# Layer hand-over of a two-layer decode kernel: a four-place weight ring, 36 instead of 72 reloaded blocks of V61, and a written-out order for layer 0's last two heads

## Chip, cores and metric

The kernel runs on one NeuronCore of a Trainium2 chip. The metric is the device time of one execution in microseconds. The engines are named as in the profile: PE (matrix multiply), PEld (its weight loads), DVE (vector), ACT (scalar), POOL (GpSimd) and SP (the queue that issues the DMAs).

## What is computed

One decode step (one token, batch 2) through two layers. Each layer is attention with 32 heads over a cache of 16384 positions, head size 128, and a small mixer with an MLP of width 4608 on a model width of 576. Both layers use the same weights and the same K and V caches.

```python
def _A_ref(x, k_cache, v_cache, wq, wo):
    q = (x @ wq).reshape(B, Sq, H, Dh).transpose(0, 2, 1, 3)
    scores = jnp.einsum("bhqd,bhkd->bhqk", q, k_cache) * (Dh ** -0.5)
    p = _softmax(scores, axis=-1)
    o = jnp.einsum("bhqk,bhkd->bhqd", p, v_cache)
    return o.transpose(0, 2, 1, 3).reshape(B, Sq, H * Dh) @ wo
...
    h = _gelu(_layernorm(x) @ w1)                 # four quarters, each shifted along the sequence
    hs = jnp.concatenate([g0, g1, g2, g3], axis=-1) @ w2
    x1 = x + hs
    return x1 + _gelu(_layernorm(x1) @ w3) @ w4

x = x + _A_ref(_layernorm(x), A_k_cache, A_v_cache, A_wq, A_wo)
x = x + _B_ref(_layernorm(x), B_w1, B_w2, B_w3, B_w4)
```

The last two lines are executed twice. With one position the shifted quarters are zero, so `hs` does not depend on x. K and V of one batch entry and head are 4 MB each; there are 64 such units, so a layer reads 512 MB of caches beside some 20 MB of weights.

## The kernel before

A unit u is one batch entry and head. Its K and V tiles are [128 partitions, 128 blocks of 128 values], 32 KB a partition. SBUF holds six such slots (`mem`); a slot is refilled as soon as the work on its old tile is done. `Store` is the planner: every transfer has a fixed address and a fixed place in one list, and `pump` issues the list strictly in order on SP, each when its address range is free.

For each unit the scores come in two ways. Half of the blocks go through PE: eight blocks (a chunk) are transposed into a PSUM buffer (`transposes`, L1246; four buffers `tps`), ACT copies them to SBUF (`evacuate`, L1258), and PE multiplies them with the query (`scores`, L1272). The other half goes through DVE: a product with the broadcast query and a sum, 16 blocks at a time (`dots`, L1292 and L1296). Then come the maximum (`softmax_max`, with an all-reduce on POOL, L1312), the exponential on ACT (`softmax_exp`), and the product with V on PE in four groups of 32 blocks (`pv`, L1366). `landed` puts a semaphore increment on POOL's queue that waits for a tile's DMA and lets PE go on; POOL runs these in program order with the all-reduces. Units 2 to 61 are a hardware loop over three units a turn; units 62 and 63 and everything between the layers are straight-line code.

Between the layers not everything is read again. Layer 1 begins with units 62, 63 and 61 (`order`): K62, V62, K63, V63 and K61 stay in SBUF, and of V61 the blocks from `GONE` on. The space of V61's first 72 blocks (four places of 576 KB, `a`) and of K61's first 36 (two places, `c`) is the ring through which wo, w3, w4 of layer 0 and wq of layer 1 are streamed: 36 pieces, most of 576 KB, wq's of 512 KB, two of w4's of 288 KB. When PE has multiplied a piece, its place is free for the piece that comes next in that place. After wq, V61's first blocks are loaded again in four pieces, then K of unit 0.

So that K62 and K63 serve layer 1 without DVE, their halves that DVE used are transposed in place (`turn`, 16 chunks: eight transposes and one evacuation each). K61's first five chunks are parked before the ring takes their space (`park`): three evacuated into the `kt` buffers, two left in PSUM buffers. Before the change four turned chunks lie in unit 63's attention and the first three parkings behind its pv of unit 62; the other twelve turns and two parkings lie between the weight pieces, after the pieces that the table `TURNS` names, and two ahead of the gelu:

```python
TURNS = {("w3", 0): 1, ("w3", 1): 1, ("w3", 2): 1, ("w4", 1): 1, ("w4", 3): 1, ("w4", 6): 1, ("w4", 8): 1,
         ("wq", 0): 1, ("wq", 1): 1, ("wq", 2): 1}
```

The order of the work between the layers is: the end of attention (`totals`, normalisation), wo (`rows_projection`, L877), layernorm (matmul of its sums L698), w3 (`cols_chunk`, L754; two of its five chunks of rows need no layernorm; tail L771), gelu, w4 (L877), layernorm, wq (L754, tail L771), and layer 1's first heads (`carried`).

Of the kernel before, what the change touches and what calls it, by code (L numbers as in the profile page):

```python
# [328 lines left out]
class KB:  # L329
    NL = 2  # L330
    CH = 8
# [6 lines left out]
    NS = 3  # L338
# [160 lines left out]
    def plan_all(self):  # L499
# [145 lines left out]
    def layer(self, l):  # L645
# [16 lines left out]
        if l == 0:  # L662
            self.turn(2, settle=False)
        self.gelu_z()
        self.settle()
# [77 lines left out]
    def cols_chunk(self, w, l, k, out, pk, n, rhs, rk, cols, first, last=False, held=False):  # L743
# [53 lines left out]
    def q_projection(self, l):  # L797
# [7 lines left out]
                       after=lambda: self.cols_chunk("wq", l, 0, acc, [ak], n, self.raw[:, 0, 0:w], "raw", cols, True, True, True))  # L805
        if l:
            self.settle()
# [56 lines left out]
    def rows_projection(self, w, l, rhs, rk):  # L864
# [4 lines left out]
        for i, (a, b, _) in enumerate(cuts):  # L869
# [16 lines left out]
            if l == 0:  # L886
                if (w, i) == ("wo", 1):
                    self.park(self.order(0)[self.U - self.CARRY - 1], self.NKT, self.PARKED)
                self.turn(self.TURNS.get((w, i), 0))

    def z_projection(self, l):
# [6 lines left out]
        chunk = lambda k: self.cols_chunk("w3", l, k, acc, [ak], MT, self.raw[:, k, :], "raw", cols, k == 0, k == R - 1, k > 0)  # L898
        chunk(0)
        self.layernorm("x1", self.x1, self.xn, "xn", after=lambda: chunk(1))  # L900
        if l == 0:
            self.settle()
# [28 lines left out]

    def still(self, l, s):

        return l == 0 and s >= self.U - self.CARRY
# [19 lines left out]
    def attention(self, l):  # L954
# [11 lines left out]
        for s in range(self.CARRY + 1 if l else 0, U):  # L966
            if s == enter:
                first = self.g.mark()
            if s == leave:
                self.g.loop(first, (leave - enter) // NS)  # L970
# [55 lines left out]
        while pend:  # L1026
            self.scores(*pend.pop(0))
# [438 lines left out]
```

## Time and profile before

| | |
|---|---|
| time, median of 3 runs (lowest to highest) | 2549.78 us (2549.26 to 2550.42) |
| the profiled execution: its time, its span | 2550.04 us, 2548.1 us |
| read from HBM | 1092.37 MB, 429 GB/s over the span |
| busy share PE, DVE, ACT, POOL | 63%, 74%, 47%, 2% |
| TensorE clock granted, mean | 0.574 |

The page of the profile counts busy time by engine, cuts the span into 40 equal slices of 63.7 us (a digit is the busy share in tenths, below them the GB/s that the DMA engines moved), follows the chain of work that ended last, and lists the costliest groups of instructions and the DMA issues with the time from issue to landing. The hand-over between the layers lies at about 1223 to 1345 us, in slices 20 to 22. Views of a window take the same trace for a stretch: busy time per engine, the instructions in order of time, who waited for whom.

### The profile page before, as it was taken

The page shows a single profiled execution, that of the slowest core. Times are in us where ns is not written, and L with a number is a line of the kernel's source. Part 1 is how long each engine was busy: PE and PEld are TensorE (multiplying, and loading weights), DVE is VectorE, ACT ScalarE, POOL GpSimd, SP SyncE. Part 2 cuts the span into 40 slices and gives each one's busy share as a digit, 9 for nine tenths or more (in the row PEclk, how much of TensorE's full clock was granted, in tenths as well). Part 3 has the DMA queues.
Part 4 walks back from the last instruction along what each step waited for, and adds up shares of the span by engine and source line. Part 5 has one row for each costly group of instructions (what it writes and reads, how often), then busy time and mean ns, then how long its engine had stood idle before and what let it go on. Part 6 is the DMA issues. An engine that isn't in the chain of part 4 may idle for free.

```text
span 2548.1 us, 74895 instructions
## 1 busy us (share of the span) xinstructions
PE 1614.3 (63%) x34407; PEld 1580.3 (62%) x34407; DVE 1896.9 (74%) x2061; ACT 1204.4 (47%) x1812; POOL 53.5 (2%) x151
## 2 busy tenths in 40 slices
PE   4666666656666666666767766666665666666566
PEld 3666666656665665666667756666665666666566
DVE  5877777777777777777638877777777777777774
ACT  3544544444454444445435544444454445444442
POOL 0000000000000000000000000000000000000000
PEclk8555555555555555555655555555555555555555
DMA  9999999999999999999999999999999999999999
GB/s 411 427 432 432 432 433 431 432 432 432 432 430 433 430 434 431 434 430 434 417 410 430 430 432 431 434 431 431 433 430 434 430 433 430 434 431 434 431 433 386
DMA packets 46928, 1093.19 MB, mean 429 GB/s; under 512 B 5140, under 2 KB 6296, under 8 KB 12440
## 3 DMA queue, kind: packets, MB, share of 16 engines
q1 hardware_dynamic: 46872, 1092.40, 100.0%
q8 instruction: 41, 0.67, 0.1%
q14 instruction: 15, 0.12, 0.0%
HBM read 1092.37 MB, written 0.00 MB: 429 GB/s over the span
## 4 chain that ended last, share of the span: by engine, by line
DMA 66%; DVE 23%; PE 5%; issue 5%; SPq 1%; ACT 0%; DVEq 0%; POOLq 0%
DMA mem<-in_A_k_cache_dram 63%; DVE s_dve L1296 12%; DVE prod L1292 9%; PE tps L1246 2%; PE mps L1366 2%; DMA mem<-in_B_w_dram 1%; DMA mem<-in_A_wo_dram 1%; PE sps L1272 1%; SPq L101 1%; PE sps L1217 1%; DVE diag L1213 0%; DMA mem<-in_A_wq_dram 0%; DVE l L1344 0%; DVE q_col L1210 0%; DVE mx L1307 0%
## 5 line engine op out<-in xcount | busy, mean ns | idle before, releaser
L1258 ACT ACTIVATE kt<-tps 128x1024 bf16<-128x1024 bf16 x992 | 1002.7, 1023 | 878.4 <-PE tps L1246 860.3
L1296 DVE TENSOR_REDUCE s_dve<-prod 128x16 f32<-128x2048 bf16 x504 | 1152.1, 2286 | 17.3
L1246 PE MATMUL tps<-ident,mem 128*128 128x128 bf16 x8192 | 999.4, 300 | 141.6 <-POOLq L202 135.2
L1292 DVE TENSOR_TENSOR prod<-mem,qb 128x2048 bf16<-128x2048 bf16 x504 | 616.8, 1224 | 525.0 <-POOLq L202 493.8
L1366 PE MATMUL mps<-p,mem 128*128 128x1 bf16 x16384 | 512.2, 165 | 549.9 <-POOLq L202 520.0
L1246 PEld LDWEIGHTS tps<-ident,mem 128*128 128x128 bf16 x8192 | 761.1, 136 | 151.6 <-POOLq L202 144.9
L1366 PEld LDWEIGHTS mps<-p,mem 128*128 128x128 bf16 x16384 | 487.6, 104 | 558.4 <-ACT p L1327 552.3
L1272 PEld LDWEIGHTS sps<-q_col,kt 128*128 128x128 bf16 x7936 | 399.1, 113 | 0.6 <-ACT kt L1258 0.5
L1272 PE MATMUL sps<-q_col,kt 128*128 128x1 bf16 x7936 | 387.6, 170 | 0.2
L1217 PE MATMUL sps<-diag,ones_bf 128*128 128x128 bf16 x127 | 36.4, 287 | 195.3 <-DVE diag L1213 195.3
L1217 PEld LDWEIGHTS sps<-diag,ones_bf 128*128 128x128 bf16 x127 | 13.2, 104 | 205.6 <-DVE diag L1213 205.6
L1321 ACT ACTIVATE mx<-mx 128x1 f32<-128x1 f32 x128 | 26.0, 203 | 235.9 <-POOL mx L1312 235.9
L1312 POOL PARTITION_ALL_REDUCE mx<-mx x128 | 51.1, 399 | 2442.2 <-DVE mx L1310 2323.5
L1220 ACT ACTIVATE qb<-sps 128x128 bf16<-128x128 f32 x127 | 35.2, 277 | 137.7 <-PE sps L1217 137.7
L1324 ACT ACTIVATE p<-s_dve,mx 128x64 bf16<-128x64 f32 x126 | 43.8, 348 | 4.1
L1258 ACT ACTIVATE mem<-tps 128x1024 bf16<-128x1024 bf16 x32 | 32.0, 1025 | 21.9 <-PE tps L1246 19.5
L1327 ACT ACTIVATE p<-sps,mx 128x64 bf16<-128x64 f32 x128 | 37.7, 294 | 0.1
L1307 DVE TENSOR_REDUCE mx<-sps 128x1 f32<-128x64 f32 x128 | 27.7, 216 | 7.3 <-PE sps L1272 7.2
L1213 DVE TENSOR_SCALAR diag<-ident,q_f 128x128 bf16<-128x128 bf16 x127 | 31.1, 245 | 0.0
L877 PE MATMUL mps<-prod,mem 128*128 128x2 bf16 x680 | 22.2, 166 | 14.1 <-DMA mem<-in_B_w_dram 8.3
L877 PEld LDWEIGHTS mps<-prod,mem 128*128 128x128 bf16 x680 | 20.6, 104 | 15.9 <-DMA mem<-in_B_w_dram 7.0
L710 ACT ACTIVATE misc<-misc 128x2 f32<-128x2 f32 x8 | 2.4, 296 | 51.8 <-DVE misc L708 51.8
(116 smaller groups left out, 293.7 us busy)
## 6 DMA issues: line engine op xcount, KB each, us to landing
mem<-in_A_k_cache_dram SPq DMA_DIRECT2D x124, 4096.0 KB, 40.7
mem<-in_A_v_cache_dram SPq DMA_DIRECT2D x123, 4096.0 KB, 49.6
mem<-in_B_w_dram SPq DMA_DIRECT2D x21, 576.0 KB, 7.8
mem<-in_B_w_dram SPq DMA_DIRECT2D x7, 1152.0 KB, 33.8
mem<-in_A_v_cache_dram SPq DMA_DIRECT2D x3, 2048.0 KB, 40.4
mem<-in_A_wq_dram SPq DMA_DIRECT2D x10, 512.0 KB, 6.6
mem<-in_A_wo_dram SPq DMA_DIRECT2D x8, 576.0 KB, 19.2
mem<-in_A_wq_dram SPq DMA_DIRECT2D x4, 1024.0 KB, 8.0
```

The costliest lines, as they stand in the source:

```text
L877: ins = pe.matmul(self.mps[:, t * B:(t + 1) * B], lhsT=buf[:, o:o + 128], rhs=rhs(k), start=(k == 0 and t == 0), stop=(k == last), skip_gr ...
L1217: self.pe(lambda pe: pe.matmul(qps, lhsT=self.ones_bf[:, :], rhs=self.diag[:, :], start=True, stop=True, skip_group_check=True), reads=["o ...
L1220: self.act(lambda e: e.activation(out=self.qb[i][:, :], in_=qps, func=ACT.Copy), reads=[("qps", i)], writes=[("qb", i)], sig=("qb", i))
L1246: ins = pe.transpose(self.tps[t][:, j * 128:(j + 1) * 128], buf[:, j * 128:(j + 1) * 128], self.ident[:, :])
L1258: self.act(lambda e: e.activation(out=out, in_=self.tps[t][:, :], func=ACT.Copy), reads=[("tps", t)], writes=keys, sig=("evac", c, t, k))
L1272: ins = pe.matmul(self.sps[sp][:, c * self.CH + j:c * self.CH + j + 1], lhsT=buf[:, j * 128:(j + 1) * 128], rhs=self.q_col[:, sp:sp + 1], ...
L1292: self.dv(lambda e: e.tensor_tensor(out=prod, in0=buf.rearrange("p (j d) -> p j d", d=128), in1=qbc, op=ALU.mult), reads=[("qb", r)] + key ...
L1296: self.dv(lambda e: e.tensor_reduce(out=sd[:, c0:c0 + DB], in_=prod, axis=AX.X, op=ALU.add), reads=["prod"], writes=[("s_dve", r)], sig=(" ...
L1312: self.pool(lambda e: e.partition_all_reduce(mx[3], mx[2], channels=128, reduce_op=ROP.max), reads=[("mx2", i)], writes=[("mx3", i)])
L1324: self.act(lambda e: e.activation(out=p[:, n:self.NB], in_=self.s_dve[i][:, 0:self.NB - n], func=ACT.Exp, bias=mx[4], scale=self.scale, ac ...
L1327: self.act(lambda e: e.activation(out=p[:, 0:n], in_=self.sps[i][:, 0:n], func=ACT.Exp, bias=mx[4], scale=self.scale, accum_out=self.ls[:, ...
L1366: ins = pe.matmul(self.mps[:, 448:449], lhsT=buf[:, j * 128:(j + 1) * 128], rhs=p[:, col:col + 1], start=b == 0, stop=b == self.NB - 1, sk ...
```

## The change

- V61: `GONE` is 36, so 92 of its 128 blocks stay and 36 are loaded again, in two pieces.
- The ring has four places, taken in turn: K61's first, V61's two, K61's second. The pieces and their sizes are the same.
- K62, K63 and V62 are loaded in two halves each (V63 was in three pieces already).
- Units 62 and 63 have an order of their own, `last_two`. Their DVE halves' turns lie there: eight chunks of K62 and four of K63, two more ahead of `totals`; two stay ahead of the gelu. All five parkings lie there too. Nothing is turned or parked between the weight pieces, and `TURNS` is gone.
- `landed` can wait for one piece alone.

```diff
@@ -339,10 +339,9 @@
     DB = 16
     PB = 32
     PARKED = 5
-    GONE = 72
+    GONE = 36
+    PLACES = 2
     RAW = 2
-    TURNS = {("w3", 0): 1, ("w3", 1): 1, ("w3", 2): 1, ("w4", 1): 1, ("w4", 3): 1, ("w4", 6): 1, ("w4", 8): 1,
-             ("wq", 0): 1, ("wq", 1): 1, ("wq", 2): 1}
...
@@ -509,17 +508,18 @@
         place = [i % 6 for i in range(len(tiles))]
         place[-1] = 2
         half, quarter = self.BP, self.BP // 2
+        fine = {("k", U - 2): (half,), ("k", U - 1): (half,), ("v", U - 2): (half,), ("v", U - 1): (half, half + quarter)}
         for (t, u), slot in zip(tiles, place):
-            self.plan_tile(t, u, slot, (half, half + quarter) if (t, u) == ("v", U - 1) else ())
...
         self.cuts = {}
         P = 4 * row
-        a, c = [4 * T + P * i for i in range(4)], [T, T + P]
-        assert 256 * self.GONE == 4 * P and 256 * 8 * self.PARKED >= 2 * P and 256 * 8 * self.NKT >= P
-        turn = iter([*a, c[0]] + [a[0], a[1], c[1], a[2], a[3], c[0]] * 6)
+        a, c = [4 * T + P * i for i in range(self.PLACES)], [T, T + P]
+        assert 256 * self.GONE == self.PLACES * P and 256 * 8 * self.PARKED >= 2 * P and 256 * 8 * self.NKT >= P
+        turn = iter([c[0], *a, c[1]] * 9)
         h = MT // 2
...
-        for i in (1, 2, 3, None, 0):
+        for i in (0, 1, None):
             if i is None:
                 self.plan_piece(*tiles[0], T, self.K[b2, h2].rearrange("(p j) d -> p (j d)", p=128), 0, quarter)
             else:
                 self.plan_piece("v", third, 4 * T, self.V[b, hh].rearrange("(p j) d -> p (j d)", p=128),
-                                i * self.GONE // 4, self.GONE // 4)
+                                i * self.GONE // self.PLACES, self.GONE // self.PLACES)
...
         self.z_projection(l)
-        if l == 0:
-            self.turn(2, settle=False)
+        turned = self.turned(2) if l == 0 else []
         self.gelu_z()
-        self.settle()
+        for at, spot in turned:
+            self.evacuate(0, at, spot)
         self.rows_projection("w4", l, lambda k: self.gT[:, k * self.B:(k + 1) * self.B], "prod")
...
-        if l == (1 if w == "wq" else 0):
-            self.turn(self.TURNS.get((w, k), 0), settle=not held)
...
-        if l:
-            self.settle()
...
-            if l == 0:
-                if (w, i) == ("wo", 1):
-                    self.park(self.order(0)[self.U - self.CARRY - 1], self.NKT, self.PARKED)
-                self.turn(self.TURNS.get((w, i), 0))
...
-                spot = self.tile(l, "k", u, b, self.CH) if still else None
-                self.evacuate(c, self.chunk, spot)
-                pend.append((s, c, self.chunk, spot))
+                self.evacuate(c, self.chunk)
+                pend.append((s, c, self.chunk, None))
...
+        self.g.loop(first, (leave - enter) // NS)
+        s, u = U - 1, o[U - 1]
+        if l:
             self.home()
-        if leave < U:
-            self.softmax_exp(l, U - 2, o[U - 2])
-            self.landed(l, "v", o[U - 2])
-        while pend:
-            self.scores(*pend.pop(0))
-        if leave < U:
-            for g in range(4):
-                self.pv(l, U - 2, o[U - 2], g)
-        s = U - 1
-        self.softmax_max(l, s, u)
-        self.keep_o(l, s - 1)
-        self.keep_l(l, s - 1)
-        if leave < U:
-            self.park(o[leave - 1], 0, self.NKT)
-        self.softmax_exp(l, s, u)
-        if leave < U:
-            self.settle()
+            while pend:
+                self.scores(*pend.pop(0))
+            self.softmax_max(l, s, u)
+            self.keep_o(l, s - 1)
+            self.keep_l(l, s - 1)
+            self.softmax_exp(l, s, u)
+        else:
+            self.last_two(o, pend)
         self.landed(l, "v", u, last=True)
         self.keep_l(l, s)
         for g in range(4):
             if g == 2:
+                if l == 0:
+                    self.turn(2)
                 self.totals(l)
             self.pv(l, s, u, g)
...
-    def turn(self, n, settle=True):
-
+    def next_chunk(self):
+
+        while self.chunk % self.NT in self.full:
+            self.chunk += 1
+        self.chunk += 1
+        return self.chunk - 1
+
+    def turn(self, n):
+
+        for at, spot in self.turned(n):
+            self.evacuate(0, at, spot)
+
+    def turned(self, n):
+
+        out = []
         for _ in range(n):
-            u, b = self.unturned.pop(0)
-            while self.chunk % self.NT in self.full:
-                self.chunk += 1
-            self.transposes(0, u, b, 0, self.chunk)
-            self.unsettled.append((self.chunk, self.tile(0, "k", u, b, self.CH)))
-            self.chunk += 1
-        if settle:
-            self.settle()
-
-    def settle(self):
-
-        while self.unsettled:
-            self.evacuate(0, *self.unsettled.pop(0))
+            s, x = self.unturned.pop(0)
+            u, at = self.order(0)[s], self.next_chunk()
+            self.transposes(0, u, x, 0, at)
+            out.append((at, self.tile(0, "k", u, x, self.CH)))
+        return out
+
+    def last_two(self, o, pend):
+
+        U, BP, PB, CH, DB = self.U, self.BP, self.PB, self.CH, self.DB
+        a, b = U - 2, U - 1
+        third = o[a - 1]
+        self.unturned = [(s, x) for s in (a, b) for h in range(2) for x in range(h * BP + PB, (h + 1) * BP, CH)]
+        self.full = ()
+        next_chunk, turn = self.next_chunk, self.turn
+
+        def chunks(s, c0, c1):
+            for c in range(c0, c1):
+                x, at = self.block(0, s, c), next_chunk()
+                self.transposes(0, o[s], x, c, at)
+                spot = self.tile(0, "k", o[s], x, CH)
+                self.evacuate(c, at, spot)
+                pend.append((s, c, at, spot))
+                if len(pend) > self.LEAD:
+                    self.scores(*pend.pop(0))
+
+        def drain():
+            while pend:
+                self.scores(*pend.pop(0))
+
+        def dots(s, i):
+            self.dots(0, s, o[s], i // 2 * BP + PB + i % 2 * DB, i * DB)
+
+        def pv(s, *groups):
+            for g in groups:
+                self.pv(0, s, o[s], g)
+
+        def keep(s):
+            self.keep_o(0, s)
+            self.keep_l(0, s)
+
+        drain()
+        self.landed(0, "k", o[a], only=0)
+        dots(a, 0)
+        chunks(a, 0, 3)
+        self.landed(0, "k", o[a], only=1)
+        self.softmax_max(0, a - 1, third)
+        keep(a - 2)
+        dots(a, 1)
+        chunks(a, 3, 4)
+        self.softmax_exp(0, a - 1, third)
+        dots(a, 2)
+        chunks(a, 4, 8)
+        self.q_broadcast(o[b], b)
+        dots(a, 3)
+        turn(2)
+        drain()
+        turn(2)
+        self.park(third, 0, self.NKT)
+        self.store.carve(("v", third, 0, self.NB), [self.GONE // self.PLACES * (i + 1) for i in range(self.PLACES)])
+        self.landed(0, "v", third)
+        self.softmax_max(0, a, o[a])
+        pv(a - 1, 0)
+        turn(2)
+        pv(a - 1, 1)
+        turn(2)
+        pv(a - 1, 2, 3)
+        self.softmax_exp(0, a, o[a])
+        self.landed(0, "k", o[b], only=0)
+        dots(b, 0)
+        chunks(b, 0, 4)
+        self.landed(0, "k", o[b], only=1)
+        dots(b, 1)
+        keep(a - 1)
+        dots(b, 2)
+        chunks(b, 4, 8)
+        dots(b, 3)
+        self.landed(0, "v", o[a], only=0)
+        turn(2)
+        drain()
+        pv(a, 0)
+        turn(2)
+        pv(a, 1)
+        self.park(third, self.NKT, self.PARKED)
+        self.landed(0, "v", o[a], only=1)
+        self.softmax_max(0, b, o[b])
+        pv(a, 2, 3)
+        keep(a)
+        self.softmax_exp(0, b, o[b])
...
@@ -1087,7 +1143,7 @@
             self.transposes(0, u, c * self.CH, c, self.chunk)
             self.store.release(("k", u, c * self.CH, self.CH))
             if c < self.NKT:
-                self.unsettled.append((self.chunk, self.chunk_place(c)))
+                self.evacuate(c, self.chunk, self.chunk_place(c))
             else:
                 self.full = (*self.full, self.chunk % self.NT)
             self.chunk += 1
...
-        assert not self.unturned and not self.unsettled
-        self.store.carve(("k", o[0], 0, self.NB), [quarter, 2 * quarter, 3 * quarter])
+        for h in range(2):
+            self.store.carve(("k", o[0], h * self.BP, self.BP), [quarter])
...
-    def landed(self, l, t, u, last=False, both=False):
+    def landed(self, l, t, u, last=False, both=False, only=None):
 
         names = [nm for nm in self.store.pieces(t, u)]
+        names = names if only is None else names[only:only + 1]
```

More of the change, by code (lines that the diff above doesn't have):

```diff
@@ L741, in unscaled, with cols_chunk @@
                 reads=["x", "raw"], writes=["raw"])
-    def cols_chunk(self, w, l, k, out, pk, n, rhs, rk, cols, first, last=False, held=False):
+    def cols_chunk(self, w, l, k, out, pk, n, rhs, rk, cols, first, last=False):
         c = rhs.shape[-1]
@@ L804, in q_projection @@
         self.layernorm("x", self.x, self.xn, "xn",
[L805 to L807 removed]
+                       after=lambda: self.cols_chunk("wq", l, 0, acc, [ak], n, self.raw[:, 0, 0:w], "raw", cols, True, True))
         be = self.coef[:, 1, :]
@@ L965, in attention @@
             self.q_broadcast(o[0], 0)
-        for s in range(self.CARRY + 1 if l else 0, U):
+        for s in range(self.CARRY + 1 if l else 0, leave):
             if s == enter:
                 first = self.g.mark()
-            if s == leave:
-                self.g.loop(first, (leave - enter) // NS)
             turning = enter <= s < leave
             u = o[s]
-            still = self.still(l, s)
             self.landed(l, "k", u, both=turning)
@@ L1006, in attention @@
                             self.keep_l(l, s - 2)
[L1007 to L1039 removed]
+                    if c == n:
+                        self.softmax_exp(l, s - 1, o[s - 1])
+                        self.landed(l, "v", o[s - 1])
+                    if 0 <= c - n < 4:
+                        self.pv(l, s - 1, o[s - 1], c - n)
+        self.g.loop(first, (leave - enter) // NS)
+        s, u = U - 1, o[U - 1]
+        if l:
+            self.home()
+            while pend:
[6 more added lines that the diff above has]
+            self.last_two(o, pend)
         self.landed(l, "v", u, last=True)
```

22 lines of the change are left out of this document (2 added, 20 removed).

## Prediction

> **What bounds the kernel now.** I read the page first: the busy shares, the forty slices, the chain that ended last.
>
> ```profile
> PE 1614.3 (63%) x34407; PEld 1580.3 (62%) x34407; DVE 1896.9 (74%) x2061; ACT 1204.4 (47%) x1812; POOL 53.5 (2%) x151
> ...
> DMA  9999999999999999999999999999999999999999
> GB/s 411 427 432 432 432 433 431 432 432 432 432 430 433 430 434 431 434 430 434 417 410 430 430 432 431 434 431 431 433 430 434 430 433 430 434 431 434 431 433 386
> ...
> HBM read 1092.37 MB, written 0.00 MB: 429 GB/s over the span
> ...
> DMA 66%; DVE 23%; PE 5%; issue 5%; SPq 1%; ACT 0%; DVEq 0%; POOLq 0%
> ```
>
> The DMA engines are busy in every slice and head the chain; no compute engine is over 74%. The time is bytes over rate. The only dips inside are slices 20 and 21 (417 and 410 GB/s), where layer 0 ends and layer 1 begins: the stretch that the change rewrites. So I took that stretch apart with a table by windows (columns: busy us and instruction count of PE, weight load, DVE, ACT, POOL; granted clock; DMA share; GB/s).
>
> ```profile
> 1264.00:1278.00 14.00, 7.73 (x193) 6.78 (x190) 1.74 (x10) 0.54 (x1) 0.00 (x0) 0.50 1.01 398
> 1278.00:1291.00 13.00, 10.92 (x208) 10.41 (x209) 5.56 (x35) 5.72 (x8) 0.00 (x0) 0.50 0.99 390
> 1291.00:1303.00 12.00, 9.68 (x217) 9.01 (x215) 1.36 (x9) 6.45 (x8) 0.00 (x0) 0.50 1.03 410
> 1303.00:1314.00 11.00, 7.06 (x156) 6.60 (x156) 3.19 (x20) 5.50 (x7) 0.00 (x0) 0.50 1.01 386
> ...
> 1400.00:1500.00 100.00, 69.43 (x1467) 68.19 (x1464) 80.94 (x82) 50.90 (x76) 1.75 (x5) 0.55 1.00 432
> ```
>
> Even here, with weights streaming through the six-place ring, the queues are full. 410 GB/s is what pieces of this size get undisturbed; 398 and 390 in the 27 us of wo and w3 are (410 - 394) / 410 x 27 = 1.05 us lost. A byte taken away here is time taken away, as long as the DMA queue does not run dry.
>
> **Part 1, the bytes.** V61 is reloaded in 36 blocks instead of 72: two pieces of 576 KB fewer, 1.18 MB. At 410 GB/s that is **-2.9 us** (432 GB/s would give -2.7, 386 -3.1).
>
> **Part 2, four places instead of six.** A place goes round like this: the piece lands, PE multiplies it, SP issues the next piece into it, that lands. These are the prices, from the issues with their time to landing (the first one of the program, on an empty queue; then the shortest seen in the ring), who SP waited for from 1264 to 1314, and PE's timeline.
>
> ```profile
> mem<-in_A_wq_dram SPq DMA_DIRECT2D x1, 1024.0 KB, 5.0
> ...
> mem<-in_A_wq_dram SPq DMA_DIRECT2D x1, 512.0 KB, 5.4
> ```
>
> ```profile
> SPq L101 <- PE mps L877: 21.2, 18, 5.5
> SPq L101 <- PE sps L754: 15.2, 13, 2.2
> ```
>
> ```profile
> 1275.97 0.70 PE L877 MATMUL mps<-prod,mem 128*128 128x2 bf16 x20 [0.72 <-DMA mem<-in_A_wo_dram]
> 1277.99 0.59 PE L698 MATMUL mps<-misc,ones_f 128*128 128x4 f32 x2 [1.33 <-DVE misc L695]
> 1278.44 1.31 PE L754 MATMUL sps<-misc,mem 128*128 128x7 bf16 x36
> ...
> 1281.41 1.31 PE L754 MATMUL sps<-misc,mem 128*128 128x7 bf16 x36
> ...
> 1302.38 0.45 PE L877 MATMUL mps<-prod,mem 128*128 128x2 bf16 x10
> 1304.16 0.59 PE L698 MATMUL mps<-misc,ones_f 128*128 128x4 f32 x2 [1.33 <-DVE misc L695]
> 1304.61 0.99 PE L754 MATMUL sps<-misc,mem 128*128 128x5 bf16 x32
> ```
>
> SP stands waiting for PE to free a place almost all the time, so the ring's size does set when transfers are issued. A 576 KB piece moves in 0.59 MB / 410 GB/s = 1.43 us. The latency around the movement: the first DMA took 5.0 us for 1.05 MB, 2.5 us of it movement, so 2.5 us is left. The other end is the ring's shortest, 5.4 - 1.3 = 4.1 us, an upper bound since it also queued behind others. A round is 1.4 + 0.7 + 2.5 = 4.6 us, 0.1 for the hand-overs: 4.7. Four places hold 4 x 1.43 = 5.7 us of movement, so **1.0 us of slack** is left, against 8.6 - 4.7 = 3.9 us with six. At 4.1 us latency the round is 6.3 us and the ring itself is too slow, by 0.6 us each time round.
>
> Now the consumer's pauses. After the last wo piece (ends 1276.67) PE starts w3 at 1278.44, 1.77 us later, where an undisturbed stream would let it start about 0.75 us later: 1.0 late, the slack exactly. The second half of w3's early chunk starts at 1281.41, 4.74 us after wo, its piece about 3.6 after wo: 1.2 late, 0.2 lost. From w4 (ends 1302.83) to wq 1.78 us again, with wq's shorter 1.27 us pieces: 0.2 lost. The gelu pause stays inside. That walk gives +0.4. But the table by windows shows 1.05 us lost even with 3.9 us of slack, so the stream is less even than my walk; I charge that loss once more and take **+1.0 us**. Ends: 0 (latency under 2) and +7.7 (4.1 us: nine rounds of 0.6, and every pause paid in full).
>
> The extras that lay between the weights (ten turned chunks, two parkings) leave this stretch. PE waits for DMA there anyway, so that is worth nothing but some of the slack, already counted by walking without them.
>
> **Part 3, the last two heads.** The ten turned chunks and two parkings move ahead of wo. The rows, one view after the other: windows, ACT's group by form in 1223.2 to 1264.3, PE's timeline, the last V63 issue with its time to landing.
>
> ```profile
> 1223.20:1264.30 41.10, 32.64 (x715) 31.52 (x715) 31.60 (x38) 26.34 (x40) 3.13 (x3) 0.67 1.00 422
> ...
> 1226.10:1229.50 3.40, 3.40 (x53) 3.40 (x52) 3.33 (x3) 3.27 (x4) 0.00 (x0) 0.50 0.94 405
> 1229.50:1232.90 3.40, 2.10 (x42) 1.93 (x39) 3.37 (x7) 3.36 (x5) 0.92 (x1) 1.00 1.01 434
> ```
>
> ```profile
> L1258 ACT ACTIVATE mem<-tps 128x1024 bf16<-128x1024 bf16 x20 | 19.8, 1026 | 9.0 <-PE tps L1246 8.6
> ```
>
> ```profile
> 1222.17 0.99 PE L1366 MATMUL mps<-p,mem 128*128 128x1 bf16 x32
> ...
> 1229.65 1.95 PE L1246 MATMUL tps<-ident,mem 128*128 128x128 bf16 x32
> ...
> 1257.33 2.72 PE L1246 MATMUL tps<-ident,mem 128*128 128x128 bf16 x24
> ...
> 1262.44 1.93 PE L1366 MATMUL mps<-p,mem 128*128 128x1 bf16 x64
> 1264.63 0.23 PE L1059 MATMUL sps<-fold,prod 128*128 128x32 bf16 x2 [0.26 <-DVE prod L1050]
> 1265.19 0.69 PE L877 MATMUL mps<-prod,mem 128*128 128x2 bf16 x20 [0.32 <-DVE prod L1063]
> ```
>
> ```profile
> 1223.19 0.33 SPq L101 DMA_DIRECT2D mem<-in_A_v_cache_dram  x1
> ...
> mem<-in_A_v_cache_dram SPq DMA_DIRECT2D x1, 1024.0 KB, 40.1
> ```
>
> V63's last quarter lands at 1223.19 + 40.1 = 1263.3, the final pv group takes half of 1.93, and wo starts at 1265.19: the end of attention hangs on V63, which stays where it is. ACT gets ten evacuations of 1.03 us: 26.3 + 10.3 = 36.6 of 41.1 us, it fits. PE gets twelve chunks of 2.72 / 3 = 0.9 us: 32.6 + 10.9 = 43.5 of 41.1 us. It does not fit at half clock. But a stretch of 3.4 us that PE filled at 0.50 was followed by one at 1.00, where four chunks took 1.95 us instead of 3.6. A PE with a backlog fills its stretches, so it gets fast ones; two give the 2.4 us back and more. The Trainium skill ("TensorE: Matmul & The Clock Gate", Part 1: The HAM clock gate) has half clock as the default and the full one after some 3.4 us of sustained work; these two rows agree.
>
> I take **+0.5 us** (wo a little late: exp of head 63 has more evacuations ahead of it on ACT). Ends: 0, and +4.1 for a clock that stays at 0.50. There I add up PE's work in the new order from 1223.2, where head 61's chunks end: 16 chunks of 0.88 with scores of 0.19 (the next rows, from the chain), 14 turns and 5 parkings of 0.9, 12 pv groups of half of 1.93 or less: 45 us, so pv ends at about 1269 and wo starts at 1269.8.
>
> ```profile
> 1225.54 0.88 PE tps L1246 x8
> 1226.41 0.19 PE sps L1272 x8
> ```
>
> The ring's four pieces have all landed by 1263.3 + 4 x 1.43 = 1269.0 then; the first place is free at 1270.5, and with 2.5 us latency DMA stands for 4.1 us.
>
> What the new order waits for: K62 and K63 come in halves, so DVE starts on a half 4.9 us earlier, which is no gain as DMA sets the end. Each `landed` on POOL stands ahead of a maximum's all-reduce: head 62's waits behind V61, head 63's behind V62's second half (a 4 MB tile, 9.7 us, before 1263.3: about 1253.5, when DVE's dots are just done). PE queues behind the diag of `q_broadcast(63)`, which follows three dots of DVE, to about 1232, about when its chunks are done. By the same addition the first ring place has its three parkings at about 1238 and the fourth (c1) its two more at about 1260; their issue is due before 1262, three pieces after V63, so SP, which issues in order, is not late. The three tiles that become two DMAs cost three issues of 0.33 us on an idle SP: nothing.
>
> **Part 4, behind the ring.** With less to reload, K1 and V0 of layer 1 come up sooner.
>
> ```profile
> 1324.36 0.33 SPq L101 DMA_DIRECT2D mem<-in_A_k_cache_dram  x1
> ...
> mem<-in_A_k_cache_dram SPq DMA_DIRECT2D x1, 4096.0 KB, 16.4
> ```
>
> ```profile
> 1335.22 0.33 SPq L101 DMA_DIRECT2D mem<-in_A_v_cache_dram  x1
> ...
> mem<-in_A_v_cache_dram SPq DMA_DIRECT2D x1, 4096.0 KB, 15.2
> ```
>
> K1 lands at 1340.8, V0 at 1350.4; each moves 4.19 MB in 9.7 us. Queued work ahead of them at issue: 1340.8 - 9.7 - 1324.4 = 6.7 and 1340.8 - 1335.2 = 5.6 us. Compute sets both issues (their slots are freed by layer 1's first heads), so 2.9 us come off: 3.8 and 2.7 us, just over the 2.5 us latency. **+0.6 us** for V0 and for V61's first piece, which now follows wq's pieces in a short ring. Ends: 0 and, at 4.1 us, +2.7.
>
> **Sum:** -2.9 + 1.0 + 0.5 + 0.6 = -0.8 us. The profiled execution took 2550.04 us (span 2548.1), 0.26 over the median of 2549.78, so the forecast is 2549.0.
>
> **Rivals.**
> 1. *The ring starves (slower).* Between the queue's 2.5 and 4.1 us the latency decides: at 3.5 the ring and its pauses cost 3.9, part 4 2.2: -2.9 + 3.9 + 0.5 + 2.2 = +3.7 (2553.5); at 4.1, -2.9 + 7.7 + 2.7 = +7.5 (2557.3). It turns slower from about 2.9 us on. For it: SP waits for PE in the whole ring. Against it: the 5.0 us row. The Trainium skill ("DMA: Bandwidth & Descriptors", anatomy of one DMA) gives a fixed part of about 2.0 us on another issue path; by that estimate the ring would lose nothing and the sum be about -1.8.
> 2. *Attention ends late:* PE stays at 0.50, -2.9 + 4.1 + 1.0 + 0.6 = +2.8, and up to +6 if ACT or POOL adds to it (2552.6 to 2556). For it: the 43.5 us against 41.1, and a ring that hides less of it. Against it: the row at 1.00.
> 3. *It all pays:* the ring evens out because PE has nothing else to do, and the 1.05 us lost now go too: -3.9 (2545.8); a little more would pass the bound.
> 4. *The saved bytes do nothing:* DMA idles before K1 and V0 for what it saved. With 3.8 and 2.7 us ahead of them that takes a latency of 5.6 us, more than any row bears; little chance by itself.
>
> **How the numbers follow.** A change within 0.2% (5.1 us) is about what a measurement of this kernel cannot tell from none. Forecast (-3 to +2): 0.53. Rival 1: 0.24, two thirds of it past +5.1 once uneven landings add to it. Rival 2: 0.14, half past it. Rival 3: 0.08, most of it past -5.1 only if layer 1's start gains as well. The last 0.01 and unforeseen delays go to slower. Faster 0.07, same 0.62, slower 0.31. The range goes from rival 3 (2545.8) to rival 1 at 4.1 us (2557.3).
>
> **What would show it.** Part 1: 1091.2 MB read. Part 2: 576 KB pieces land in 5 to 6 us instead of 7.8, and the windows of wo to wq stay at 385 to 410 GB/s; at 360 or less rival 1 holds. Part 3: wo's first matmuls by 1266 and clock 1.00 in more of 1223 to 1264; after 1269 rival 2 holds. Part 4: no DMA gap of over 1 us before K1 and V0. The forecast is wrong if the queue's latency under load is not near 2.5 us, or if an order on POOL, ACT or PE that I took for covered holds back the last pv.

## The result, with the profile after

The changed kernel takes 2560.56 us (median of 6 runs, 2557.91 to 2562.32), beside 2549.66 us (2549.24 to 2550.42) for the kernel before on the same chip: 10.9 us longer, a ratio of 1.0041 with a 95% interval of 1.0032 to 1.0051. The forecast was 2549.0 with a range up to 2557.3, so the time lies outside it. The profiled execution took 2561.79 us, span 2559.8 (before 2548.1).

First the page of the kernel after: the forty slices (now of 64 us), the bytes read, the chain that ended last, and the issues into the ring with their median time to landing.

```profile
GB/s 409 429 430 433 432 431 432 432 431 432 431 433 431 433 430 432 432 432 430 403 332 428 432 433 431 431 433 432 430 433 434 429 432 433 432 430 433 433 429 386
...
HBM read 1091.19 MB, written 0.00 MB: 426 GB/s over the span
...
DMA 65%; DVE 22%; PE 5%; issue 5%; ACT 1%; SPq 1%; DVEq 0%; POOLq 0%
...
mem<-in_B_w_dram SPq DMA_DIRECT2D x21, 576.0 KB, 6.4
...
mem<-in_A_wq_dram SPq DMA_DIRECT2D x10, 512.0 KB, 6.3
```

The bytes fell as planned, DMA still heads the chain (65%), and the loss is in one place: the slice that holds most of the weight ring moves 332 GB/s instead of 410. The same stretch by windows (busy us and count of PE, weight load, DVE, ACT, POOL; granted clock; DMA share; GB/s) shows that every stretch of the ring is hit, and that the loss stops where the ring stops:

```profile
1264.00:1278.00 14.00, 6.70 (x203) 6.01 (x203) 1.40 (x5) 1.36 (x2) 0.00 (x0) 0.50 0.93 334
1278.00:1291.00 13.00, 6.41 (x149) 5.82 (x146) 6.08 (x38) 1.87 (x3) 0.00 (x0) 0.50 0.93 339
1291.00:1303.00 12.00, 6.85 (x145) 6.15 (x146) 1.77 (x12) 3.78 (x5) 0.00 (x0) 0.50 0.90 312
1303.00:1314.00 11.00, 4.49 (x124) 4.08 (x124) 1.83 (x13) 0.54 (x2) 0.00 (x0) 0.50 0.87 288
1314.00:1326.00 12.00, 3.81 (x108) 3.29 (x106) 1.49 (x8) 1.24 (x2) 0.00 (x0) 0.50 0.85 283
1326.00:1340.00 14.00, 9.41 (x337) 9.16 (x336) 11.45 (x12) 2.88 (x6) 2.50 (x2) 0.50 1.03 400
```

Before, the first four of these stretches had 398, 390, 410 and 386 GB/s. Now neither side is busy: the DMA engines stand for up to 15% of the time (share 0.85), and PE works for a third to a little over half of it. In the timeline of PE (start, busy time, work; in brackets how long PE stood idle and for whom) the idle time before a piece jumps between two kinds of values:

```profile
1266.43 1.95 PE L873 MATMUL mps<-prod,mem 128*128 128x2 bf16 x60 [0.32 <-DVE prod L1031]
...
1271.99 0.69 PE L873 MATMUL mps<-prod,mem 128*128 128x2 bf16 x20 [0.73 <-DMA mem<-in_A_wo_dram]
...
1277.75 0.69 PE L873 MATMUL mps<-prod,mem 128*128 128x2 bf16 x20 [2.07 <-DMA mem<-in_A_wo_dram]
...
1299.58 0.69 PE L873 MATMUL mps<-prod,mem 128*128 128x2 bf16 x20 [2.38 <-DMA mem<-in_B_w_dram]
...
1307.68 0.69 PE L873 MATMUL mps<-prod,mem 128*128 128x2 bf16 x20 [2.56 <-DMA mem<-in_B_w_dram]
```

0.7 us is an even stream (pieces 1.4 us apart, 0.7 us of work); 2 to 2.6 us is a piece that came 1.4 to 1.9 us late. About every third piece of the ring is late in this way.

Where the time goes can be added up from the landings. wq's last piece and K of unit 1, issue and time to landing, before:

```profile
1306.93 0.33 SPq L101 DMA_DIRECT2D mem<-in_A_wq_dram  x1
```

```profile
mem<-in_A_wq_dram SPq DMA_DIRECT2D x1, 512.0 KB, 7.2
```

and after (the timeline of SP, then the landing times of those issues; the third issue group is the two pieces of V61, the first of which took 3.6 us):

```profile
1320.10 0.33 SPq L101 DMA_DIRECT2D mem<-in_A_wq_dram  x1
...
1323.91 1.57 SPq L101 DMA_DIRECT2D mem<-in_A_v_cache_dram  x2
...
1335.97 0.33 SPq L101 DMA_DIRECT2D mem<-in_A_k_cache_dram  x1
```

```profile
mem<-in_A_wq_dram SPq DMA_DIRECT2D x1, 512.0 KB, 5.6
...
mem<-in_A_v_cache_dram SPq DMA_DIRECT2D x1, 576.0 KB, 3.6
...
mem<-in_A_k_cache_dram SPq DMA_DIRECT2D x1, 4096.0 KB, 15.1
```

wq's last piece lands at 1325.7 instead of 1314.1: +11.6 us, 11.5 of it gathered since wo's first piece, which lands at 1264.9 (before 1264.7). K of unit 1 lands at 1351.1 instead of 1340.8: +10.3. So what lies behind the ring gains 1.3 us. The shift of 10.3 us stays through layer 1 to its last V. The weights behind that add another 1.4 us in the profiled execution (its span is 11.7 us longer), which lies 1.2 us over the median.

### The profile page after: what moved, and what is told of

The parts are those of the page before. It is cut to its first block, busy times and chain, and to the rows that moved or that the text cites. A ratio compares the mean times of both kernels' runs of the same rounds, so it can differ in the third digit from the quotient of the medians.

```text
span 2559.8 us, 74900 instructions
## 1 busy us (share of the span) xinstructions
PE 1610.2 (63%) x34407; PEld 1575.1 (62%) x34407; DVE 1896.9 (74%) x2061; ACT 1202.9 (47%) x1812; POOL 52.5 (2%) x151
## 3 DMA queue, kind: packets, MB, share of 16 engines
HBM read 1091.19 MB, written 0.00 MB: 426 GB/s over the span
## 4 chain that ended last, share of the span: by engine, by line
DMA 65%; DVE 22%; PE 5%; issue 5%; ACT 1%; SPq 1%; DVEq 0%; POOLq 0%
DMA mem<-in_A_k_cache_dram 62%; DVE s_dve L1353 12%; DVE prod L1349 9%; DMA mem<-in_B_w_dram 2%; PE mps L1423 2%; PE tps L1303 2%; SPq L101 1%; ACT mem L1315 1%; DMA mem<-in_A_wo_dram 1%; PE sps L1329 1%; PE sps L1274 1%; DMA mem<-in_A_wq_dram 0%; DVE diag L1270 0%; DVE q_col L1267 0%; DVE l L1401 0%
## 6 DMA issues: line engine op xcount, KB each, us to landing
mem<-in_A_wo_dram SPq DMA_DIRECT2D x8, 576.0 KB, 10.9
```

## Experiments

Two theories. **A, the short ring:** four places hold too little of the stream, whatever the order of attention. **B, the new order:** the rearranged heads leave wo's stream or PE's code worse off, whatever the ring. Later the question was what in a round of a place is longer than the prediction had it. "Ring time" below is from the landing of wo's first piece to that of wq's last, 36 pieces, and "round" is ring time / 35 x places: the mean time from one issue into a place to the next. Both come from one profiled execution of each kernel; the kernel after and fetch4, which differ by idle waits on POOL alone, have 60.9 and 58.3 us, so a difference of two or three microseconds between ring times says little by itself. The before column is the kernel before beside it on the same chip.

| kernel | places | us | before | ratio, 95% interval | ring time | round |
|---|---|---|---|---|---|---|
| before | 6 | 2549.66 | | | 49.4 | 8.5 |
| after | 4 | 2560.56 | 2549.66 | 1.0041 (1.0032 to 1.0051) | 60.9 | 7.0 |
| ring6 | 6 | 2549.85 | 2549.85 | 1.0000 (0.9990 to 1.0009) | 48.5 | 8.3 |
| ring5 | 5 | 2553.16 | 2549.85 | 1.0013 (1.0003 to 1.0022) | 52.4 | 7.5 |
| before_ring4 | 4 | 2559.02 | 2549.85 | 1.0032 (1.0019 to 1.0045) | 58.1 | 6.6 |
| half4 | 8 halves | 2557.30 | 2549.85 | 1.0028 (1.0018 to 1.0039) | 56.2 | |
| half6 | 12 halves | 2551.67 | 2549.68 | 1.0008 (0.9998 to 1.0018) | 51.2 | |
| fetch4 | 4 | 2560.65 | 2549.68 | 1.0044 (1.0027 to 1.0061) | 58.3 | 6.7 |
| fetch6 | 6 | 2549.96 | 2549.68 | 1.0001 (0.9991 to 1.0010) | 48.6 | 8.3 |
| nopause4 | 4 | 2559.19 | 2549.68 | 1.0035 (1.0023 to 1.0048) | 57.7 | 6.6 |
| nopause6 | 6 | 2549.75 | 2550.05 | 0.9999 (0.9989 to 1.0008) | 48.6 | 8.3 |
| quick4 | 4 | 2556.94 | 2550.05 | 1.0028 (1.0017 to 1.0040) | 54.6 | 6.2 |

### The new order with the old ring, and with one place less

ring6 is the kernel after with six places and 72 reloaded blocks; everything of the last two heads' order stays.

```diff
-    GONE = 36
-    PLACES = 2
+    GONE = 72
+    PLACES = 4
...
-        for i in (0, 1, None):
+        for i in (0, 1, 2, 3, None):
```

> The changed kernel with two more ring places (six, as before; V61 again reloaded in 72 blocks), the new order of the last two heads kept. Theory A, the short ring: the loss of 11 us comes from a ring of four places that leaves the DMA engines without queued work, so with six it goes away: 2549 to 2551 us. Theory B, the new order of the last two heads (wo starts 1.2 us later, more work ahead of it): the loss stays and two more pieces are loaded, about 2563 us.

ring5 is the same with `GONE = 54`, `PLACES = 3` and `(0, 1, 2, None)`.

> The changed kernel with one more ring place (five; 54 blocks of V61 reloaded, 0.59 MB or 1.4 us more than with four). Theory A: the loss falls steeply with the slack of a round (1.0 us with four places, 2.4 with five, 3.9 with six), so 2551 to 2554 us. Theory B: about 2562 us.

ring6 takes 2549.85 us, what the kernel before takes beside it; the stream is whole again. The first four stretches by windows, ring6 and then ring5:

```profile
1264.00:1278.00 14.00, 6.98 (x207) 6.13 (x204) 1.63 (x9) 0.95 (x1) 0.00 (x0) 0.50 1.02 400
1278.00:1291.00 13.00, 8.21 (x179) 7.74 (x180) 5.99 (x39) 2.14 (x4) 0.00 (x0) 0.50 1.00 392
1291.00:1303.00 12.00, 7.33 (x190) 6.58 (x188) 1.56 (x10) 3.52 (x4) 0.00 (x0) 0.50 1.03 407
1303.00:1314.00 11.00, 5.18 (x138) 4.63 (x139) 2.98 (x18) 1.78 (x3) 0.00 (x0) 0.50 1.03 396
```

```profile
1264.00:1278.00 14.00, 6.51 (x190) 5.66 (x187) 1.66 (x10) 0.71 (x1) 0.00 (x0) 0.50 1.00 385
1278.00:1291.00 13.00, 7.36 (x171) 6.89 (x172) 5.26 (x34) 1.87 (x3) 0.00 (x0) 0.50 0.99 370
1291.00:1303.00 12.00, 6.97 (x168) 6.42 (x165) 1.71 (x12) 3.78 (x5) 0.00 (x0) 0.50 0.98 362
1303.00:1314.00 11.00, 4.96 (x130) 4.38 (x130) 3.32 (x20) 1.78 (x3) 0.00 (x0) 0.50 0.97 358
```

Theory B falls: the order alone costs nothing that can be measured. One place less costs 3.3 us (theory A had 2551 to 2554 us), although it saves half of the bytes that the change saves; a second one costs another 7.4 (2560.56 - 2553.16). The loss is steep and begins at five places.

### The old order with four places

before_ring4 is the kernel before with its own order, its turns between the weight pieces and 36 reloaded blocks.

```diff
-    GONE = 72
+    GONE = 36
...
-        turn = iter([*a, c[0]] + [a[0], a[1], c[1], a[2], a[3], c[0]] * 6)
+        turn = iter([*a, c[0]] + [a[0], a[1], c[1], c[0]] * 9)
...
-        for i in (1, 2, 3, None, 0):
+        for i in (1, None, 0):
```

> The kernel before with the four-place ring alone (36 blocks of V61 reloaded), its own order of the last heads with the turns and parkings between the weights. Theory A: slower than the changed kernel or like it, 2560 to 2566 us, since the turns lie in the ring's round and the fourth place comes only after the second wo piece. Theory B: the bytes saved show, about 2547 us.

It takes 2559.02 us; its stretch from 1303 to 1326 us, by windows:

```profile
1303.00:1314.00 11.00, 6.85 (x144) 6.14 (x142) 2.28 (x15) 2.91 (x4) 0.00 (x0) 0.50 0.90 318
1314.00:1326.00 12.00, 7.08 (x184) 6.52 (x185) 2.11 (x10) 4.27 (x6) 0.00 (x0) 0.50 0.89 303
```

So the short ring alone, in either order, makes the loss. The old order's turns between the pieces, for which 2560 to 2566 us were expected, did not make it worse than the kernel after; the two intervals overlap.

### Half-size pieces

half4 is the kernel after with every place cut in two: wo in pieces of two rows, w3 and wq in quarters of a row chunk. The trace shows 70 pieces in the place of 36 (16 of wo, 17 of w3, 20 of w4, 17 of wq; the two tails keep a whole place).

```diff
-        turn = iter([c[0], *a, c[1]] * 9)
+        full = [c[0], *a, c[1]]
+        turn = iter([x + y for x in full for y in (0, P // 2)] * 16)
...
-        self.cuts["wo", 0] = [(i, i + 4, next(turn)) for i in range(0, 32, 4)]
+        self.cuts["wo", 0] = [(i, i + 2, next(turn)) for i in range(0, 32, 2)]
...
-        self.groups = [(0, 4, 8, 12, 16, 18), (0, 8, 12, 16, 18)]
+        self.groups = [(0, 2, 4, 6, 8, 9, 11, 13, 15, 17, 18), (0, 8, 12, 16, 18)]
```

> The changed kernel with the same ring space cut into eight places of half the size (68 pieces, of 256 to 288 KB, in place of 36; descriptors of half the length). A round is shorter by half a movement and half a multiplication, about 1.0 us, so the slack is 2.0 instead of 1.0 us with the same bytes. Theory A: half or more of the loss comes back, 2550 to 2555 us. Theory B: about 2560 us. If short descriptors or the number of issues (68 of 0.4 us) are a price of their own, it is over 2560 us.

half6 is half4 with six whole places (`GONE = 72`, `PLACES = 4`), to see what the smaller pieces cost by themselves.

> Six places cut into twelve of half the size, new order, 72 blocks of V61 reloaded. Against the six-place ring (2549.85 us) a round is 1.0 us shorter and the first piece is free earlier. If the six-place ring still loses to unevenness (393 to 396 GB/s in it against 410 to 418 undisturbed): -1 to -2 us, 2548 to 2549. If not: 2550 us, or more if the issues or the short descriptors cost.

With four places the halves win back 3.3 us (2557.30 against 2560.56), less than the half of the loss or more that was expected of them. With six they take 2.0 us more than the kernel before beside them, where a gain or nothing was expected, but the interval reaches below 1, so this loss is not clear of noise. The likely reason for the gain is that the same space, given back in smaller steps, keeps more of the stream under way. It does not repair it: half4's stretches, where the kernel after had 334, 339, 312 and 288 GB/s, are

```profile
1264.00:1278.00 14.00, 7.96 (x214) 6.77 (x213) 1.82 (x8) 1.36 (x2) 0.00 (x0) 0.50 0.95 333
1278.00:1291.00 13.00, 6.70 (x150) 5.76 (x150) 5.65 (x36) 1.87 (x3) 0.00 (x0) 0.50 1.02 377
1291.00:1303.00 12.00, 7.84 (x171) 7.10 (x171) 1.77 (x12) 3.78 (x5) 0.00 (x0) 0.50 1.00 354
1303.00:1314.00 11.00, 4.80 (x117) 4.14 (x118) 3.32 (x20) 1.78 (x3) 0.00 (x0) 0.50 0.93 324
```

### Instruction fetches

The engines' code comes over the same DMA engines (the instruction queue of the page). Each fetch of 16 KB takes 0.9 to 1.1 us of one engine. In the packets of the kernel after, all six of them in the ring are followed within 3.5 us by a piece that lands more than 2 us after the one ahead of it; four more such late pieces follow no fetch. In ring6 six such fetches run beside the ring too, and only one piece, at its start, is late. fetch4 is the kernel after, and fetch6 is ring6, with several hundred waits on POOL that are met at once, meant to make POOL's code longer and so add fetches beside the ring.

```diff
         self.landed(l, "v", u, last=True)
+        if l == 0:
+            for i in range(768):
+                self.g.op("gpsimd", lambda e: e.wait_ge(self.g.dma_sems["xin"], 16))
```

> The changed kernel, with 768 empty waits (on a semaphore long since reached) on POOL's idle queue while the ring runs: 48 KB more of code, three more instruction fetches of 16 KB, each of which holds one of the 16 DMA engines for about 1.1 us. Nothing waits for them. If a fetch costs its whole time in a short ring, because the weight piece lands only when the slowest engine is done: +3 us on the changed kernel, about 2563.5 us. If fetches are absorbed: 2560.5 us.

> The same 768 waits in the six-place ring with the new order (2549.85 us without them). If a longer queue lets the other engines run ahead while one fetches, so that fetches on different engines overlap: at most +1 us, 2549.9 to 2550.9. If a fetch costs its time whatever the ring: +3 us, 2553.

Neither moved. This says little, since the lines added only 384 instructions and three fetches of 8 KB. quick4, below, shows late pieces without a fetch. What share of the loss in the kernel after the six fetches make is open.

### The consumer's pauses

nopause4 takes out what lies between the products of layer 0's attention and layer 1's first heads; w3, w4 and wq are streamed as before.

```diff
+        if l == 0:
+            self.straight()
+            return
...
+    def straight(self):
...
+        for k in range(KT - 1):
+            self.cols_chunk("w3", 0, k, out, [pk], MT, self.ident[:, 0:B], "ident", cols, k == 0)
...
+        self.rows_projection("w4", 0, lambda k: self.ident[:, 0:B], "ident")
```

> The changed kernel without the consumer's pauses: between attention and the next layer's query both layernorms, the gelu and all their small steps are left out, and w3, w4 and wq are multiplied with a constant instead of the activations; every piece is loaded and multiplied as before, in the same four places. If the pauses (two layernorms, gelu, layernorm) make the loss of the short ring: near -2 against the kernel before, 2548 to 2551 us. If the ring is too short even for an undisturbed consumer (uneven engines, fetches): most of the loss stays, 2555 to 2558 us.

nopause6 is the same with six places.

> nopause4 with six places and 72 reloaded blocks (layernorms, mixer's shift term and gelu between layer 0's attention and layer 1's first heads left out; w3, w4 and wq are streamed and multiplied with a constant). With six places the ring already keeps 396 GB/s with the pauses in, so without them: 2548 to 2549.9 us, 0 to -2 us against ring6 (2549.85), ring stretch 47 to 48.5 us. That makes the price of four places without any pause of layernorm or gelu about 9 to 11 us. If the pauses were a cost of their own, apart from the ring, this kernel would gain as much as nopause4 did or more: 2547 us or less.

nopause4's ring by windows, without a pause and still short of the full rate:

```profile
1264.00:1278.00 14.00, 7.12 (x214) 6.35 (x213) 1.82 (x9) 0.00 (x0) 0.00 (x0) 0.50 0.95 352
1278.00:1291.00 13.00, 5.96 (x144) 5.31 (x144) 0.53 (x4) 0.00 (x0) 0.00 (x0) 0.50 0.97 354
1291.00:1303.00 12.00, 6.62 (x146) 6.12 (x146) 1.06 (x7) 5.00 (x6) 0.00 (x0) 0.50 0.91 303
1303.00:1314.00 11.00, 4.06 (x116) 3.57 (x117) 0.66 (x4) 0.00 (x0) 0.00 (x0) 0.50 0.92 323
```

Without any pause four places still cost 9.4 us (2559.19 - 2549.75), more than the 2555 to 2558 us expected; with the pauses it was 10.7 (2560.56 - 2549.85). So the steady stream makes most of the loss. The 1.3 us between the two, for layernorms and gelu, are not clear of noise: the intervals of nopause4 and of the kernel after overlap.

### A shorter hold by PE

quick4 is nopause4 with only a fifth of the matmuls of most ring pieces; the DMAs are the same.

```diff
-                    for t in range(KT):
+                    for t in range(KT if l else 1):
...
-                for m in range(lo, hi):
+                for m in range(lo, hi, 5 if (w, l) != ("wq", 0) and l == (w == "wq") else 1):
```

> nopause4 (four places, no layernorm, no gelu) with only about a fifth of the matmuls for each weight piece of the ring left in, so PE holds a piece for 0.15 to 0.2 us instead of 0.7: every round of a place is about 0.55 us shorter, the DMAs are the same. If the lookahead in time decides (slack 1.0 us becomes 1.5), this lies between four and five places: ring5 had 2.4 us of slack and lost about 10 us less in the ring than four places with the same pauses, so 0.5 us more should give back 3 to 5 us: 2554 to 2556 us, ring stretch 53 to 55 us against 57.7. If the number of pieces that are under way decides and not PE's share of the round: 2559 us again. If the transfers alone were uneven, whatever the slack: also 2559 us.

The ring time falls from 57.7 to 54.6 us, inside the 53 to 55 expected if slack decides. The run takes 2.2 us less than nopause4, 0.9 us more than the 2556 expected at most, and the two intervals overlap, so this points to slack without proving it. (The 10 us that ring5 was said to lose less in the ring are 60.9 - 52.4 = 8.5.) Four places can even keep up for a while: from 1278 to 1291 us the stream runs at full rate, and then it breaks and does not come back.

```profile
1264.00:1278.00 14.00, 3.31 (x62) 2.37 (x59) 1.48 (x10) 0.00 (x0) 0.00 (x0) 0.50 0.97 349
1278.00:1291.00 13.00, 3.55 (x55) 2.98 (x56) 0.00 (x0) 0.00 (x0) 0.00 (x0) 0.50 1.01 401
1291.00:1303.00 12.00, 3.30 (x42) 2.64 (x39) 1.05 (x7) 5.00 (x6) 0.00 (x0) 0.50 0.97 351
1303.00:1314.00 11.00, 1.84 (x27) 1.27 (x28) 0.66 (x4) 0.00 (x0) 0.00 (x0) 0.50 0.91 313
```

In PE's timeline of quick4 a piece of the even stretch, and then three that come late:

```profile
1285.05 0.29 PE L771 MATMUL sps<-ident,mem 128*128 128x2 bf16 x4 [1.14 <-DMA mem<-in_B_w_dram]
...
1299.05 0.27 PE L899 MATMUL mps<-ident,mem 128*128 128x2 bf16 x4 [2.27 <-DMA mem<-in_B_w_dram]
...
1308.76 0.27 PE L771 MATMUL sps<-ident,mem 128*128 128x2 bf16 x4 [2.48 <-DMA mem<-in_A_wq_dram]
...
1316.81 0.27 PE L771 MATMUL sps<-ident,mem 128*128 128x2 bf16 x4 [2.58 <-DMA mem<-in_A_wq_dram]
```

From 1296 to 1320 us the DMA queues of quick4 hold the ring's packets alone, with no row for the instruction queue:

```profile
q1 hardware_dynamic: 2067, 7.60, 90.7%
```

The last fetch before that began at 1292.5 and took 1.0 us. It may still have had a part in the late piece at 1299, but the next two, 15 and 23 us behind it, need no instruction fetch. This break comes where the ring holds less: w4's two pieces of 288 KB and wq's of 512 KB each take a whole place. That is where the break lies; that the smaller filling causes it was not tried by itself.

## Why the prediction was wrong

**Part 1, the bytes:** the count was right: 1091.19 MB were read against 1091.2 foretold. What they were worth stands under part 4.

**Part 3, the last two heads:** right in mechanism. wo's first matmul starts at 1266.43 (before 1265.19), 1.2 us later where +0.5 was taken and past the 1266 that was named as the sign. But wo's first piece lands where it did, and ring6 shows the whole part to be worth 0.0 us (ratio 0.9990 to 1.0009). The rule taken from the two rows of before, that a filled stretch at 0.50 is followed by one at 1.00, held well enough here to carry twelve more chunks: from 1223.2 to 1264.3 the mean clock rose from 0.67 to 0.79 and PE was busy for 35.2 us, not 43.5.

```profile
1223.20:1264.30 41.10, 35.19 (x767) 33.41 (x768) 28.56 (x35) 33.27 (x50) 2.09 (x3) 0.79 0.99 419
```

This also takes rival 2 away: attention did not end late.

**Part 4, behind the ring:** right in direction, 1.0 us off in size. The bytes less 0.6 us made -2.3; K of unit 1 came only 1.3 us nearer to wq's last piece. Where the other 1.0 us went is not shown.

**Part 2, the ring:** here it failed. The term was +1.0 us; the ring time grew by 11.5 us (60.9 - 49.4). The step that failed is "A round is 1.4 + 0.7 + 2.5 = 4.6 us, 0.1 for the hand-overs: 4.7", with the 1.0 us of slack that follows. The ring's own rounds are 7.0 us with four places and 7.5 with five. At the rate of ring6 (48.5 / 35 = 1.39 us per piece) four places hold 5.5 us, five 6.9 and six 8.3, so five are just too few and four far too few. These rounds are worked out from the ring times and only tell the loss once more; the cause lies in what a round is made of.

What in the round was too small can be told from the runs. PE's hold was right (0.69 us in the rows). So was the latency on a nearly empty queue: 3.6 us for V61's first piece, less 1.4 us of movement, leaves 2.2, a little under 2.5. The pauses are not it: without them the round is 6.6 us, against 7.0 and 6.7 in the two traces with them (after, fetch4). A hold that is 0.4 us shorter went with a round 0.4 us shorter (quick4, 6.2). What is left is the DMA itself, from issue to landing. The median of w3's and w4's 576 KB pieces between 1265 and 1326 us, in the kernel after and then in ring6:

```profile
mem<-in_B_w_dram SPq DMA_DIRECT2D x17, 576.0 KB, 6.1
```

```profile
mem<-in_B_w_dram SPq DMA_DIRECT2D x17, 576.0 KB, 7.5
```

With six places over half of the 7.5 us is waiting (a piece with almost nothing ahead of it took 3.6), which costs nothing while the stream is whole. With four it is 6.1, where the prediction put 1.4 + 2.5 = 3.9. The trace shows where these 2.2 us lie. A piece's semaphore rises once for each of the 16 DMA engines, and the trace keeps the time of every rise; the piece has landed at the last one. For V61's first piece the 16 rises come 3.25 to 3.64 us after the issue, all within 0.4 us. For the 32 pieces issued into the ring of the kernel after from 1265 us on, the first rise comes after 3.7 us in the median, as for the lone piece, and the last is 2.3 us behind the first. So the foremost engine does what the prediction had all of them do, and the piece waits for the hindmost, for which the round had no term.

The trace of before has the same spread: 2.1 us in the median. It is harmless there, since the first rise comes after 4.6 us: even the foremost engine still had work queued. In the stretch of quick4 that runs at full rate the spread is 1.3 us and the pieces land 5.5 us after their issue; at its late pieces it is 2.1 to 3.3. The Trainium skill ("DMA: Bandwidth & Descriptors", Why a DMA increments its semaphore by 16 and not by 1) states that these engines finish independently and all must have reported; the spread in these traces agrees.

What drives the engines apart is known in part. Two pieces of the kernel after that land late behind an instruction fetch (at 1286.8 and 1299.5) have 15 rises within 1.2 and 1.4 us, and the last one 1.4 and 1.6 us later, so one engine alone holds them up. Slow packets add to it: the first 12 packets of V61's first piece take 0.3 to 1.0 us instead of 0.18, and from 1265 to 1314 us 6.6% of the 4608-byte packets take over 0.3 us, before 1.6%. How much each contributes stays open.

The Trainium skill ("DMA: Bandwidth & Descriptors", Anatomy of one DMA) gives a fixed cost of about 2.0 us on another issue path, close to the 2.2 seen on the nearly empty queue. But the sum of about -1.8 that it led to is off by more than 12 us: here the time of one DMA alone did not give that of a piece in the stream.

The two safeguards of the step failed with it. "I charge that loss once more" took the 1.05 us that an uneven stream costs with 3.9 us of slack as its cost with 1.0 us; but six places had one late piece where four had ten (ring6 and the kernel after, under Instruction fetches). And the upper end, 5.4 - 1.3 = 4.1 us of latency, was the shortest of a kind taken as the worst: it bounds the best piece, not the typical one. So rival 1's outcome came, at a size beyond its price at 4.1 us (2557.3). Its condition, and the last line of the prediction, a latency under load that is not near 2.5 us, was met in the ring (6.1 - 1.4 = 4.7 us), though not on the nearly empty queue (2.2). Of the signs named beforehand, the windows answered at once (283 to 339 where "at 360 or less rival 1 holds"). The other sign, pieces that land in 5 to 6 us instead of 7.8, nearly came true (6.1) and did not mean that the ring was well: a landing time falls when less is queued, whether or not the stream is whole. By the prediction's own 5.7 us for four places, less 0.8 for PE and the hand-overs, the pieces of a whole stream would have landed in 4.9 us.

Rivals 3 and 4 fell: the 1.05 us lost in wo and w3 did not come back, and behind the ring the saved bytes did give something.

No kernel tried beats the one before. ring6 equals it, and with pauses taken out as well (nopause6) its ring time stays at 48.6 us, so six places leave little to gain in this ring.

## What to carry to other kernels

Size a streaming ring by what a piece takes in the loaded stream, up to its last DMA engine, and not by the latency of one DMA on an empty queue. Here the prediction's 3.9 us for a lone piece, the 2.1 us between the engines in the trace of before and 0.8 for PE and the hand-overs make 6.8 us, an estimate that the trace of before allowed. Four places hold 5.5 us, and six, with 8.3, were enough. Price unevenness by what is left of the slack, since a deep ring can absorb what a shallow one cannot; and take the upper end of a latency from median or long landings, not from the shortest. A few saved megabytes (2.9 us by the prediction, 1.3 as measured) were not worth two places of this ring.

## What was unexpected of the hardware

- Cutting pieces from 576 to 288 KB helps a starved ring (3.3 us of 10.9) and does not help a fed one (2551.67 against 2549.68 beside it; the loss is not clear of noise).
- The 16 DMA engines finish a piece 2.1 us apart in the median even in the stream of before, which runs at 386 to 410 GB/s; for V61's first piece, nearly alone on the queue, they are within 0.4 us.
- In the one trace of quick4 a four-place stream is whole for some 20 us and then breaks and does not recover: 401 GB/s from 1278 to 1291, then 351 and 313. The last instruction fetch began at 1292.5, well ahead of two of its three late pieces.
- A late piece of the kernel after is 1.4 to 1.9 us late in the rows shown, as long as or longer than a piece's whole movement of 1.4 us.
